# Weight products of a one-core decode block: the weights as moving operand in four column tiles, c loaded as rows, a 256 KB last load

## The chip, the cores and the metric

The kernel runs on one core of one Trainium2 chip. The metric is the device time of one execution in microseconds (us), lower is better. A median is given with the lowest and the highest run. A profiled execution has a span, from its first to its last instruction; the time is some 1.8 us longer than the span of the same execution (426.25 and 424.5 us before).

Engines: PE = TensorE (matmul), PEld = its weight loads, DVE = VectorE, ACT = ScalarE, POOL = GpSimd, SP = SyncE.

## The reference, cut to what matters

```
mod = (silu(c) @ w_mod)                          # c [2, 1024], w_mod [1024, 6144], bf16
sa, ca, ga, sb, cb, gb = six parts of mod
h = layernorm(x) * (1 + ca) + sa                 # x [2, 1, 1024]
q = h @ wq                                       # wq [1024, 4096]
o = softmax(q @ K^T * 128**-0.5) @ V             # caches [2, 4, 32768, 128], 32 query heads
x = x + ga * (o @ wo)                            # wo [4096, 1024]
h = layernorm(layernorm(x) * (1 + cb) + sb)
x = x + gb * (gelu(h @ w1 + b1) @ w2 + b2)       # w1 [1024, 3584], w2 [3584, 1024]
```

Each batch row gives one token, so every product with a weight matrix has only two rows. The caches are 134 MB and the weights 44 MB: everything is read once, and there is little to compute on it.

## The kernel before

A single stream of loads of 1 to 2 MB fills a ring of buffers in the on-chip memory. SP issues them in a fixed order, each as soon as its place in the ring is free. The stages are: w_mod (8 loads), wq (4), K and V (64), wo (4), w1 (4), w2 (4). Loads of the weights, and the order of w_mod's rows:

```
    wm_v = w_mod.rearrange("(p k) n -> p k n", k=KT8)
    for k in range(KT8):
        add(("wmod", k), [6 * DM], wm_v[:, k, :], k * 12 * KB)
    # ... wq, K and V, wo, w1
    w2_v = B_w2.rearrange("(q p j) n -> p q (j n)", p=128, j=4)
    for k, off in enumerate((80, 112, 128, 144)):
        lo, hi = 2 * k, min(2 * k + 2, 7)
        add(("w2", k), [hi - lo, 4 * DM], w2_v[:, lo:hi, :], off * KB)   # three of 2 MB, the last 1 MB
```

c is loaded so that each of the 128 partitions gets its own 16 bytes of each row. The weights are the stationary operand of each matmul, in blocks of 128 by 128, and the two columns of the input are moved past them. The result stands in columns, which is the form that the next stage wants:

```
    T.dma("act", lambda e: e.dma_start(c_sb[:, :, :], c.rearrange("b (p k) -> p b k", k=KT8)), ...)

    for k in range(KT8):                                   # w_mod; wq, wo and w1 alike
        for j in range(NMOD):                              # 48
            pe(lambda e, ...: e.matmul(psS[0][:, 2 * j:2 * j + 2], lhsT=w[:, j * 128:(j + 1) * 128], rhs=siluT[:, :, k], ...))

    for q in range(7):                                     # w2, the end of the kernel
        it = need("w2", q // 2)
        for j in range(4):
            for k in range(KT8):
                pe(lambda e, ...: e.matmul(psO[:, 2 * k:2 * k + 2], lhsT=w[:, q % 2, j * DM + k * 128:j * DM + (k + 1) * 128],
                                           rhs=gT[:, 4 * q + j, :], ...))
    dve(mT = psO * mod(5));  dve(res_bf = mT + x1b)        # shortened
    pe(turn res_bf into rows);  dve(copy to res16);  store
```

## Time and profile before

| | before |
|---|---|
| median, lowest to highest | 426.06 us, 426.01 to 426.18 (3 runs) |
| span of the profiled execution | 424.5 us |
| read from memory | 178.28 MB, 420 GB/s over the span |
| last load has landed / end of the span | 420.48 / 424.5 us |

No engine is busy for more than 68%, but the DMA engines are 90% busy or more in every slice except the first and the last. The loads bound the kernel. Two queues carry instructions rather than data: 16 packets of 16 KB on one, and 8 packets of 8 KB on the other.

The costliest groups, two weight stages of before (line, engine, operation, output <- input, shape, count | busy us, mean ns of one | idle time before them and its releaser):

```profile
L448 PE MATMUL psS<-siluT,wmod 128*128 128x2 bf16 x384 | 11.0, 165 | 8.6 <-DMA wmod<-in_w_mod_dram 8.6
...
L647 PE MATMUL psO<-gT,w 128*128 128x2 bf16 x224 | 6.6, 165 | 9.5 <-DMA w<-in_B_w_dram 9.5
```

The idle time of PE in both stages ends with a load.

Windows of 1 us at the end of before. Columns: window, its length, then busy time and count of PE, PEld, DVE, ACT and POOL, granted clock of PE, DMA share, GB/s.

```profile
416.00:417.00 1.00, 0.00 (x0) 0.00 (x0) 0.00 (x0) 0.00 (x0) 0.00 (x0) 0.50 0.89 369
417.00:418.00 1.00, 0.00 (x0) 0.00 (x0) 0.00 (x0) 0.00 (x0) 0.00 (x0) 0.50 0.61 246
418.00:419.00 1.00, 0.91 (x34) 0.91 (x35) 0.00 (x0) 0.00 (x0) 0.00 (x0) 0.50 0.50 213
419.00:420.00 1.00, 0.96 (x36) 0.87 (x33) 0.00 (x0) 0.00 (x0) 0.00 (x0) 0.50 0.24 98
```

The DMA share falls from 0.89 to 0.24 before the last load is complete. The engines do not finish together. The page counts 16 DMA engines, and in this trace each large load shows 16 semaphore increments at different times; here each is read as one engine's end. The offsets of those of the last w2 load, in us after the first of them, sorted (worked out from the semaphore records of the trace):

```
before, first at 416.79: 0 .1 .2 .3 .4 .8 1.6 1.9 3.0 3.1 3.1 3.2 3.2 3.2 3.2 3.7
```

The first w_mod load has a spread of 0.35 us, this one 3.7 us. PE waited for the last of the 16: its products of the third w2 load started at 418.09 us and those of the last at 420.52 us, each 0.04 to 0.05 us after the 16th increment (418.04 and 420.48 us). The end of the chain of waits of before (start us, us, what):

```profile
391.30 29.17 DMA w<-in_B_w_dram
420.48 0.05 issue
420.52 1.03 PE psO L647 x32
...
421.57 0.18 DVE mT L651
...
421.78 0.24 DVE res_bf L652
...
422.07 0.29 PE psM L653
...
422.38 0.28 DVE res L655
```

After the last landing at 420.48 us come 32 matmuls, four small steps and the store. From here on, "tail" is the time from the last landing to the end of the span: 4.0 us in before. So the span is last landing plus tail, and each part can be read alone.

### The profile page before, as it was taken

Reading aid. Unit: us, or ns where it says so; the run is one execution under the profiler, and the core shown is the slowest. Engines: PE = TensorE matmul, PEld = TensorE weight load, DVE = VectorE, ACT = ScalarE, POOL = GpSimd, SP = SyncE. Lnnn points to the kernel's source line nnn. Section 1 sums busy time; section 2 is a strip of 40 time slices with the busy share of each in tenths; the row PEclk is TensorE's granted clock in tenths of the full one; section 3 lists DMA queues with packets and bytes.
Section 4 is the critical chain, followed back from the end, with each engine's and each line's share of the span. In section 5 each row is a group of like instructions: output and inputs, shape, how many; then the busy total and the mean of one; then the engine's idle time right before and its main releaser. Section 6 shows DMA issues by size and latency. Waiting matters only on the chain.

```text
span 424.5 us, 13364 instructions
## 1 busy us (share of the span) xinstructions
PE 287.6 (68%) x6035; PEld 252.8 (60%) x6035; DVE 162.8 (38%) x340; ACT 155.1 (37%) x266; POOL 2.8 (1%) x17
## 2 busy tenths in 40 slices
PE   0633369768997789578867857895878681544644
PEld 0633368766875778477766837784867661243643
DVE  0200027535674466146535624661555343102100
ACT  1100016428556348143734543481438335100100
POOL 1000000000000000000000000000000000000000
PEclk9999999969999889888969898897889886855555
DMA  8999999999999999999999999999999999999994
GB/s 329 429 425 422 435 426 426 431 424 433 428 434 429 434 431 430 431 431 432 432 432 429 433 426 435 428 432 432 429 434 428 432 432 430 431 428 420 426 427 176
DMA packets 14470, 178.61 MB, mean 421 GB/s; under 512 B 1767, under 2 KB 1774, under 8 KB 2798
## 3 DMA queue, kind: packets, MB, share of 16 engines
q1 hardware_dynamic: 14112, 178.27, 98.6%
q8 instruction: 16, 0.26, 0.2%
q10 hardware_dynamic: 334, 0.02, 0.1%
q14 instruction: 8, 0.07, 0.0%
HBM read 178.28 MB, written 0.00 MB: 420 GB/s over the span
## 4 chain that ended last, share of the span: by engine, by line
DMA 79%; PE 17%; ACT 1%; SPq 1%; DVE 1%; issue 1%; DVEq 0%; ACTq 0%
DMA K<-in_A_k_cache_dram 59%; PE psKT L477 11%; DMA wo<-in_A_wo_dram 8%; DMA w<-in_B_w_dram 7%; DMA wmod<-in_w_mod_dram 5%; PE psS L489 3%; PE psO L519 1%; SPq L374 1%; ACT KT_sb L481 1%; ACT E_sb L510 0%; PE psS L613 0%; PE psO L647 0%; ACT L510 0%; DVE KT_sb L483 0%; PE psM L423 0%
## 5 line engine op out<-in xcount | busy, mean ns | idle before, releaser
L477 PE MATMUL psKT<-ident,K 128*128 128x128 bf16 x2048 | 175.5, 238 | 39.7 <-DMA K<-in_A_k_cache_dram 39.7
L477 PEld LDWEIGHTS psKT<-ident,K 128*128 128x128 bf16 x2048 | 134.5, 106 | 50.3 <-DMA K<-in_A_k_cache_dram 46.2
L481 ACT ACTIVATE KT_sb<-psKT 128x1024 bf16<-128x1024 bf16 x96 | 97.8, 1019 | 169.5 <-PE psKT L477 169.3
L483 DVE COPY KT_sb<-psKT 128x1024 bf16<-128x1024 bf16 x160 | 108.3, 689 | 117.4 <-PE psKT L477 116.2
L489 PE MATMUL psS<-qcur,KT_sb 128*128 128x8 bf16 x2048 | 88.8, 168 | 10.8 <-ACT KT_sb L481 7.1
L489 PEld LDWEIGHTS psS<-qcur,KT_sb 128*128 128x128 bf16 x2048 | 80.1, 99 | 16.5 <-ACT KT_sb L481 9.3
L519 PE MATMUL psO<-V,E_sb 128*32 128x512 bf16 x512 | 34.4, 394 | 4.1 <-DMA V<-in_A_v_cache_dram 3.3
L510 ACT ACTIVATE E_sb<-S_sb,negm 128x256 bf16<-128x256 f32 x64 | 32.3, 505 | 9.7 <-DVE negm L506 8.8
L494 DVE TENSOR_REDUCE m1c<-S_sb 128x8 f32<-128x512 f32 x32 | 21.9, 686 | 16.4 <-ACT S_sb L493 15.1
L493 ACT ACTIVATE S_sb<-psS 128x512 f32<-128x512 f32 x32 | 19.0, 593 | 15.0 <-PE psS L489 15.0
L519 PEld LDWEIGHTS psO<-V,E_sb 128*32 128x32 bf16 x512 | 11.3, 98 | 14.3 <-DMA V<-in_A_v_cache_dram 4.1
L448 PE MATMUL psS<-siluT,wmod 128*128 128x2 bf16 x384 | 11.0, 165 | 8.6 <-DMA wmod<-in_w_mod_dram 8.6
L448 PEld LDWEIGHTS psS<-siluT,wmod 128*128 128x128 bf16 x384 | 10.8, 104 | 9.0 <-DMA wmod<-in_w_mod_dram 9.0
L456 PE MATMUL psO<-hT,wq 128*128 128x2 bf16 x256 | 7.5, 165 | 12.5 <-DMA wq<-in_A_wq_dram 12.5
L613 PE MATMUL psS<-atT,wo 128*128 128x2 bf16 x256 | 7.5, 165 | 12.2 <-DMA wo<-in_A_wo_dram 12.2
L613 PEld LDWEIGHTS psS<-atT,wo 128*128 128x128 bf16 x256 | 7.1, 104 | 13.1 <-DMA wo<-in_A_wo_dram 13.1
L456 PEld LDWEIGHTS psO<-hT,wq 128*128 128x128 bf16 x256 | 7.1, 104 | 12.8 <-DMA wq<-in_A_wq_dram 12.8
L425 ACT ACTIVATE stat<-stat 128x2 f32<-128x2 f32 x3 | 0.6, 203 | 36.9 <-DVE stat L424 36.9
L647 PE MATMUL psO<-gT,w 128*128 128x2 bf16 x224 | 6.6, 165 | 9.5 <-DMA w<-in_B_w_dram 9.5
L647 PEld LDWEIGHTS psO<-gT,w 128*128 128x128 bf16 x224 | 6.3, 104 | 9.8 <-DMA w<-in_B_w_dram 9.8
L510 ACT ACTIVATION_READ_ACCUMULATOR E_sb<-S_sb,negm 128x1 f32 x64 | 12.1, 189 | 0.0
L629 PE MATMUL psS<-h2T,w 128*128 128x2 bf16 x224 | 7.8, 172 | 3.1 <-DMA w<-in_B_w_dram 1.9
(85 smaller groups left out, 85.7 us busy)
## 6 DMA issues: line engine op xcount, KB each, us to landing
K<-in_A_k_cache_dram SPq DMA_DIRECT2D x32, 2048.0 KB, 31.8
V<-in_A_v_cache_dram SPq DMA_DIRECT2D x32, 2048.0 KB, 35.4
wmod<-in_w_mod_dram SPq DMA_DIRECT2D x8, 1536.0 KB, 18.0
wq<-in_A_wq_dram SPq DMA_DIRECT2D x4, 2048.0 KB, 37.8
wo<-in_A_wo_dram SPq DMA_DIRECT2D x4, 2048.0 KB, 27.3
w<-in_B_w_dram SPq DMA_DIRECT2D x4, 1792.0 KB, 37.7
w<-in_B_w_dram SPq DMA_DIRECT2D x3, 2048.0 KB, 30.8
w<-in_B_w_dram SPq DMA_DIRECT2D x1, 1024.0 KB, 29.2
```

What stands on the lines that cost most here:

```text
L448: pe(lambda e, w=it.view, j=j, k=k: e.matmul(psS[0][:, 2 * j:2 * j + 2], lhsT=w[:, j * 128:(j + 1) * 128], rhs=siluT[:, :, k], start=(k == ...
L456: pe(lambda e, w=it.view, h=h, k=k: e.matmul(psO[:, 2 * h:2 * h + 2], lhsT=w[:, k % 2, h * 128:(h + 1) * 128], rhs=hT[:, k, :], start=(k = ...
L477: pe(lambda e, kq=kq, jj=jj, w=it.view, t=t: e.transpose(psKT[kq][:, jj * 128:(jj + 1) * 128], w[:, t, :], ident[:, :]), reads=[it.reg, "i ...
L481: act(lambda e, src=src: e.activation(KT_sb[g8][:, :, :], src, ACT.Copy), reads=[f"psKT{kq}"], writes=[f"KT_sb{g8}"], sem=f"ev{cc}_{g8}")
L483: dve(lambda e, src=src: e.tensor_copy(KT_sb[g8][:, :, :], src), reads=[f"psKT{kq}"], writes=[f"KT_sb{g8}"], sem=f"ev{cc}_{g8}")
L489: pe(lambda e, t=t, jj=jj: e.matmul(ps[:, t * HPG:(t + 1) * HPG], lhsT=KT_sb[g8][:, jj, :], rhs=qcur[:, :], start=True, stop=True), reads= ...
L493: act(lambda e: e.activation(Sc, ps[:, :].rearrange("p (t h) -> p h t", h=HPG), ACT.Copy), reads=[preg], writes=[f"S_sb{i % 2}_{cc}"], sem ...
L494: dve(lambda e: e.tensor_reduce(m1c[:, :, cc], Sc, AX.X, ALU.max), reads=[f"S_sb{i % 2}_{cc}"], writes=[f"m1c{cc}"])
L510: act(lambda e: e.activation(E_sb[:, :, h, :], S_sb[j][:, h, :].rearrange("p (u t) -> p u t", t=4), ACT.Exp, bias=negm[:, h:h + 1], scale= ...
L519: pe(lambda e, t4=t4, tg=tg, q=q: e.matmul(psO[32 * q:32 * q + 32, :], lhsT=E_sb[:, tg // 4, :, :].rearrange("p h t -> p (h t)"), rhs=it.v ...
L613: pe(lambda e, w=it.view, g=g, j=j, k=k: e.matmul(psS[0][:, 2 * k:2 * k + 2], lhsT=w[:, j, k * 128:(k + 1) * 128], rhs=atT[g][:, j, :], st ...
L647: pe(lambda e, w=it.view, q=q, j=j, k=k: e.matmul(psO[:, 2 * k:2 * k + 2], lhsT=w[:, q % 2, j * DM + k * 128:j * DM + (k + 1) * 128], rhs= ...
```

## The change

The intent: make the weights the moving operand, 512 columns at a time, against a stationary operand of 32 columns, of which two hold the input. Four such products go to four column tiles of the array at once. This cuts PE's instructions for the weights from 1,344 matmuls to 360. In the P.V stage of before (line 519), which had this form already, four matmuls start within about 10 ns of each other at clock 1.0 (12 ns at most), and within 14 ns at 0.5; a group of four follows the last after 216 ns and 426 ns (medians).

The price is that results come as rows. In this kernel they are copied out of PSUM and turned into columns by matmuls with a small selection matrix, in float32 except for q. The core of the diff (declarations, padding of the inputs to 32 columns, wq and w1 cut):

```diff
-    wm_v = w_mod.rearrange("(p k) n -> p k n", k=KT8)
+    wm_v = w_mod.rearrange("(k p) n -> p k n", k=KT8)
 ...
-    for k, off in enumerate((80, 112, 128, 144)):
-        lo, hi = 2 * k, min(2 * k + 2, 7)
-        add(("w2", k), [hi - lo, 4 * DM], w2_v[:, lo:hi, :], off * KB)
+    for k, off in enumerate((80, 112, 128)):
+        add(("w2", k), [2, 4 * DM], w2_v[:, 2 * k:2 * k + 2, :], off * KB)
+    add(("w2", 3), [3 * DM], w2_v[:, 6, 0:3 * DM], 144 * KB)
+    add(("w2", 4), [DM], w2_v[:, 6, 3 * DM:4 * DM], 150 * KB)
 ...
-    T.dma("act", ... c_sb[:, :, :], c.rearrange("b (p k) -> p b k", k=KT8)), key="ld_c", ...)
+    T.dma("act", ... c16[:, :], c.rearrange("b (k p) -> (b k) p", p=128)), key="ld_c", ...)
 ...
     for k in range(KT8):
         it = need("wmod", k)
-        for j in range(NMOD):
-            pe(... e.matmul(psS[0][:, 2 * j:2 * j + 2], lhsT=w[:, j * 128:(j + 1) * 128], rhs=siluT[:, :, k], ...)
+        for ch in range(12):
+            n, q = ch // 4, ch % 4
+            pe(... e.matmul(bank[n][32 * q:32 * q + 32, :], lhsT=inT[:, k, :], rhs=w[:, ch * 512:(ch + 1) * 512], ...)
+    # three copies of 512 columns to SBUF, 12 float32 matmuls that turn them into columns
 ...
-    for q in range(7):
+    for q in range(6):
         it = need("w2", q // 2)
         for j in range(4):
-            for k in range(KT8):
-                pe(... e.matmul(psO[:, 2 * k:2 * k + 2], lhsT=w[:, q % 2, ...], rhs=gT[:, 4 * q + j, :], ...)
+            for hf in range(2):
+                t = 2 * (j % 2) + hf
+                pe(... e.matmul(psS[0][32 * t:32 * t + 32, :], lhsT=gT[:, 4 * q + j, :],
+                                rhs=w[:, q % 2, j * DM + hf * 512:j * DM + (hf + 1) * 512], ...)
+    load_row("dve", psS[0], "psS0", 3)
+    for j in range(4):                                    # the last 1 MB in the old form
+        it = need("w2", 3 if j < 3 else 4)
+        if j == 3:
+            to_columns(psO, "psO", 3, False, False)       # turn of w2's row: four float32 matmuls
+        for k in range(KT8):
+            pe(... e.matmul(psO[:, 2 * k:2 * k + 2], lhsT=w[:, lo:lo + 128], rhs=gT[:, 24 + j, 0:2], ...)
```

The two bias loads also move, from the start to after the attention loop, and one of them is split in four.

## The prediction

> What bounds the kernel. The load stream: the page gives 178.28 MB read at 421 GB/s, and its DMA row is 9 in every slice but the first and the last; the windows view gives 427 to 432 GB/s from 40 us to 415 us. Loads are issued some 31 us ahead (K), so no compute stage starves the queue: PE is 35 to 60% busy in the weight stages, waiting for a load each time. Only three things move the time: when the stream starts, how evenly its 16 engines finish, and what follows the last landing.
>
> 1. Even finish. In the windows view the DMA share falls to 0.89, 0.61, 0.50, 0.24 in the single microseconds from 416 to 420. The semaphore increments of the last w2 load run from 416.79 to 420.48 us. This spread is 0.3 us at first (wmod 0) and grows by about 1.5 us on one engine after each 16 KB packet of the instruction queue (16 on the page). At the end eight engines stand at 0 to 0.8 us or with one fetch at 1.6 to 1.9, the rest with two at 3.0 to 3.7: fetches go round about eight engines. Counted from the built programs, PE has about 4,095 instructions of 64 B, 16 pages of 16 KB; after, about 2,250, 8.8 pages (weight matmuls fall from 1,344 to 360). With 8 fetches, one per engine, I expect a spread of 1.6 to 2.2 us and the last landing 1.6 us earlier (1.3 to 2.0).
>
> 2. Head. c as 256 packets of 16 B lasts until 10.6 us, [...] but costs each engine only 0.15 to 0.3 us. Gain 0.2 us. PE starts wmod at 6 us instead of 15.7: worth nothing, the ring is prefilled.
>
> 3. PE in the weight stages. Old: 64 weight loads in 1.79 us. New: 16 matmuls of 512 columns; the same form in the last P.V stage (line 519) takes 427 ns per four at clock 0.5, 216 at 1.0. So 1.7 us per 2 MB against a load every 4.9 us: worth nothing. [...] Row copies and float32 turns add some 3 us after wo and 5 us after w1 (a float32 pass is 0.23 us at clock 0.5, line 418); gT comes near 411.5 instead of 406.7, after w2's first landing, but PE catches up before the third. Off the critical path.
>
> 4. Tail. Before, 32 matmuls follow the last landing (1.05 us); the end comes 4.0 us after it. After, 8 follow, but the turn of w2's row stands before them in PE's order: the third w2 load lands 2.4 us before the last, its 16 matmuls end 0.5 us before it, the copy of 512 float32 takes about 0.6 us (estimate from the 0.69 us reduction of line 494), then four float32 matmuls, eight passes of 0.23 us, 1.8 us. PE ends 2.3 us after the last landing instead of 1.1: plus 1.2 us (0.8 less if the clock is up).
>
> Sum: -0.2 - 1.6 + 1.2 = -0.6 us: 425.4 us, range 423.9 to 426.8. Faster by over 2%: 0.01; within: 0.98; slower: 0.01.
>
> What would show it: 8 or 9 instruction-queue packets instead of 16 (DMA queues); DMA share near 1 until 416.5, dropping faster (windows); last w2 landing near 418.6; the chain of waits ending in the turn of w2's row, not in a load.
>
> Wrong if: two fetches fall on one engine (1.4 us slower), the clock rises in w2 (0.8 faster), the turn is hidden, or the late bias loads put engines behind.

What the trace of before shows for some of its figures: c's 256 packets of 16 bytes took 9 ns each, which is 0.14 us for each of 16 engines if they were spread evenly (an estimate from these figures); 16 packets of 16 KB over the 4,095 counted instructions give 64 B for one; and at line 418 a float32 matmul stands as two passes that start 0.23 us apart at clock 0.5. The 0.8 us for a higher clock was the author's estimate.

## More of the kernel before

DVE's other work, which matters later: in each of the eight attention rounds DVE copies 20 of the 32 groups of turned K out of PSUM (`EVAC_PATTERN`, five of eight), ACT the other 12. DVE also takes the maximum of the scores, in four parts and once more over the four.

From the page of the kernel before: its span; busy time of each engine, share of the span and count of instructions; DMA share in 40 slices, in tenths (9 is 90% or more); two of the DMA queues with packets, MB and share; and bytes read.

```profile
span 424.5 us, 13364 instructions
PE 287.6 (68%) x6035; PEld 252.8 (60%) x6035; DVE 162.8 (38%) x340; ACT 155.1 (37%) x266; POOL 2.8 (1%) x17
...
DMA  8999999999999999999999999999999999999994
...
q8 instruction: 16, 0.26, 0.2%
...
q14 instruction: 8, 0.07, 0.0%
HBM read 178.28 MB, written 0.00 MB: 420 GB/s over the span
```

## The result, and the profile after

Ratios here and below are the mean time of one kernel's fast runs over the mean of the other's fast runs of the same rounds, so they are not quite the ratio of the medians quoted.

| | before | after |
|---|---|---|
| median, lowest to highest (4 runs each) | 426.03 us, 425.90 to 426.18 | 427.38 us, 427.30 to 427.42 |
| ratio to before, 95% interval | | 1.0031, 1.0014 to 1.0049 |
| span of the profiled execution | 424.5 us | 425.5 us |
| last landing | 420.48 us | 420.21 us |
| tail, last landing to end | 4.0 us | 5.3 us |

The kernel is 1.35 us slower, within 2%, and outside the predicted range of 423.9 to 426.8 us. In the profiled executions the last landing came 0.27 us sooner and the tail became 1.3 us longer. The page after:

```profile
span 425.5 us, 11554 instructions
PE 301.5 (71%) x5116; PEld 236.0 (55%) x5116; DVE 166.9 (39%) x347; ACT 156.8 (37%) x269; POOL 4.9 (1%) x23
...
q8 instruction: 9, 0.15, 0.1%
q14 instruction: 8, 0.07, 0.0%
```

The 16 KB instruction packets fell from 16 to 9, as predicted (the ninth came after the last landing). The 8 KB packets remained 8. PE became busier (301.5 us against 287.6), not less busy. The groups of the new weight stages:

```profile
L451 PE MATMUL psS<-wmod,inT 128*32 128x512 bf16 x64 | 8.0, 593 | 13.4 <-DMA wmod<-in_w_mod_dram 13.4
L641 PE MATMUL psS<-wo,atT 128*32 128x512 bf16 x64 | 7.6, 627 | 12.0 <-DMA wo<-in_A_wo_dram 12.0
```

PE still waits for the load in these stages; the form of the product is worth nothing there. The windows at the end:

```profile
416.00:417.00 1.00, 0.00 (x0) 0.00 (x0) 0.00 (x0) 0.00 (x0) 0.00 (x0) 0.50 0.84 346
417.00:418.00 1.00, 0.23 (x4) 0.14 (x8) 0.00 (x0) 0.00 (x0) 0.00 (x0) 0.50 0.62 250
418.00:419.00 1.00, 1.00 (x12) 0.33 (x8) 0.00 (x0) 0.00 (x0) 0.00 (x0) 0.50 0.24 94
419.00:420.00 1.00, 1.00 (x22) 0.39 (x15) 0.28 (x1) 0.00 (x0) 0.00 (x0) 0.50 0.06 23
```

In the last of these microseconds the DMA share is 0.06, that is one engine of sixteen. The increments of the last load show the same:

```
before, first at 416.79: 0 .1 .2 .3 .4 .8 1.6 1.9 3.0 3.1 3.1 3.2 3.2 3.2 3.2 3.7
after,  first at 416.64: 0 .2 .4 .5 .8 .8 1.6 1.6 1.8 1.9 2.1 2.1 2.1 2.2 2.5 3.6
```

The seven engines at 3.0 to 3.2 us are gone, as wanted. One engine at 3.6 us has remained, and it is the one that the last load waits for. The chain of waits after:

```profile
387.77 29.96 DMA w<-in_B_w_dram
417.73 0.04 issue
417.77 1.93 PE psS L708 x15
...
419.72 0.70 DVE S_sb L650
...
420.47 1.87 PE psO L654 x8
422.34 0.23 PE psO L719 x8
...
422.59 0.19 DVE mT L722
```

The chain no longer goes back to the last load, which lands at 420.21 us. It comes from the third w2 load (417.73) over 16 matmuls, the copy of the row and its turn. The turn's eight float32 passes last until 422.34 us; only then come the eight matmuls for the last 256 KB. PE's last product ends 2.34 us after the last landing, against 1.07 us in before.

### The profile page after: what moved, and what is told of

The parts are those of the page before. It is cut to its first block, busy times and chain, and to the rows that moved or that the text cites. A ratio compares the mean times of both kernels' runs of the same rounds, so it can differ in the third digit from the quotient of the medians.

```text
span 425.5 us, 11554 instructions
## 1 busy us (share of the span) xinstructions
PE 301.5 (71%) x5116; PEld 236.0 (55%) x5116; DVE 166.9 (39%) x347; ACT 156.8 (37%) x269; POOL 4.9 (1%) x23
## 4 chain that ended last, share of the span: by engine, by line
DMA 79%; PE 18%; ACT 1%; SPq 1%; issue 0%; DVE 0%; DVEq 0%
DMA K<-in_A_k_cache_dram 59%; PE psKT L500 11%; DMA wo<-in_A_wo_dram 8%; DMA w<-in_B_w_dram 7%; DMA wmod<-in_w_mod_dram 5%; PE psS L512 3%; PE psO L542 1%; SPq L377 1%; ACT KT_sb L504 1%; PE psS L708 0%; PE psS L641 0%; PE psO L654 0%; ACT E_sb L533 0%; DVE S_sb L650 0%; PE psM L523 0%
## 5 line engine op out<-in xcount | busy, mean ns | idle before, releaser
L500 PE MATMUL psKT<-ident,K 128*128 128x128 bf16 x2048 | 173.4, 236 | 36.8 <-DMA K<-in_A_k_cache_dram 34.4
L500 PEld LDWEIGHTS psKT<-ident,K 128*128 128x128 bf16 x2048 | 132.6, 106 | 48.7 <-DMA K<-in_A_k_cache_dram 42.0
L542 PE MATMUL psO<-V,E_sb 128*32 128x512 bf16 x512 | 39.0, 435 | 5.3 <-DMA V<-in_A_v_cache_dram 4.6
L451 PE MATMUL psS<-wmod,inT 128*32 128x512 bf16 x64 | 8.0, 593 | 13.4 <-DMA wmod<-in_w_mod_dram 13.4
L641 PE MATMUL psS<-wo,atT 128*32 128x512 bf16 x64 | 7.6, 627 | 12.0 <-DMA wo<-in_A_wo_dram 12.0
L472 PE MATMUL psS<-wq,inT 128*32 128x512 bf16 x64 | 7.5, 627 | 7.0 <-DMA wq<-in_A_wq_dram 6.0
L451 PEld LDWEIGHTS psS<-wmod,inT 128*32 128x32 bf16 x64 | 1.2, 108 | 19.0 <-DMA wmod<-in_w_mod_dram 18.8
L641 PEld LDWEIGHTS psS<-wo,atT 128*32 128x32 bf16 x64 | 1.8, 128 | 16.7 <-DMA wo<-in_A_wo_dram 14.6
L650 DVE COPY S_sb<-psS 128x512 f32<-128x512 f32 x2 | 1.4, 692 | 22.1 <-PE psS L641 13.0
L563 PE MATMUL psM<-msum,hmat 128*128 128x128 f32 x16 | 4.2, 346 | 7.5 <-DVE msum L557 7.5
L459 DVE COPY S_sb<-psS 128x512 f32<-128x512 f32 x1 | 0.7, 692 | 21.5 <-PE psS L451 21.5
```

Source lines behind the costliest of these rows:

```text
L451: pe(lambda e, w=it.view, k=k, ch=ch, n=n, q=q: e.matmul(bank[n][32 * q:32 * q + 32, :], lhsT=inT[:, k, :], rhs=w[:, ch * 512:(ch + 1) * 512],
L472: pe(lambda e, w=it.view, k=k, ch=ch, n=n, q=q: e.matmul(bank[n][32 * q:32 * q + 32, :], lhsT=inT[:, k, :], rhs=w[:, k % 2, ch * 512:(ch + ...
L500: pe(lambda e, kq=kq, jj=jj, w=it.view, t=t: e.transpose(psKT[kq][:, jj * 128:(jj + 1) * 128], w[:, t, :], ident[:, :]), reads=[it.reg, "i ...
L542: pe(lambda e, t4=t4, tg=tg, q=q: e.matmul(psO[32 * q:32 * q + 32, :], lhsT=E_sb[:, tg // 4, :, :].rearrange("p h t -> p (h t)"), rhs=it.v ...
L641: pe(lambda e, w=it.view, g=g, j=j, hf=hf, q=q: e.matmul(psS[0][32 * q:32 * q + 32, :], lhsT=atT[g][:, j, :], rhs=w[:, j, hf * 512:(hf + 1 ...
```

## The theory, and how pages are followed

The result leaves two questions: whether the turn is the whole loss in the tail, and which engine it is that ends last.

*Instruction pages.* The trace of before shows packets of the kind "instruction" while the kernel runs: 16 of 16 KB, at 21.1 to 421.5 us, and 8 of 8 KB, at 88.9 to 354.4 us. One such packet is called a page here. The built programs have about 4,095 PE instructions before and 2,250 after, and the page of each kernel shows 16 and 9 packets of 16 KB: in before that is one for 256 instructions, and 2,250 would be 8.8 of these. So they are read as PE's. The 8 KB packets are read as pages of the other engines. At the start of four of them DVE's count of records in the trace is 65, 200, 329 and 453 in before, and 67, 197, 328 and 456 in after, so one comes about every 128 instructions. The author's estimate from this is the 64th, the 192nd, the 320th and the 448th. Three belong to ACT in the same way (its records then count 67, 203 and 319 in before). The one left, at 354.4 us, fits neither count and is put down to SP.

*What a page costs.* The offset of an engine can be followed from load to load, because the increments of successive loads keep their order until something delays one engine. In before and after a PE page put one engine about 1.5 us behind (in before from 1.59 to 3.15 us, seen at the landing at 381.3 us), a DVE page about 0.95 us (list below), an ACT page about 0.65 us (in before from 0.83 to 1.48 us at 210.7 us, and from 1.37 to 2.01 us at 293.3 us). The delay stayed, but for a drift of some 0.1 us (in before from 2.10 us at 166.9 us to 2.01 us at 244.7 us), while the stream didn't pause. The clearest trace is the experiment old_row_order below, where one engine shows four jumps:

```
old_row_order: DVE pages fetched at 83.7, 159.9, 239.2, 318.4 us
               jumps of one engine, seen at the landings at 87.5, 165.5, 244.1, 322.7 us: 1.06 0.95 0.96 0.90
before:        DVE pages fetched at 88.9, 163.3, 243.7, 323.6 us
               jumps of one engine, seen at the landings at 94.1, 166.9, 249.6, 327.9 us: 0.95 0.97 0.96 0.94
after:         DVE pages fetched at 84.9, 160.5, 239.1, 318.4 us
               jumps of one engine, seen at the landings at 87.8, 165.7, 244.1, 322.7 us: 0.97 0.97 0.97 0.95
```

So in these runs PE's pages went round about eight engines, but DVE's all fell on the same one. Four of them make about 3.8 us. The limit of this: packets in the trace do not name their DMA engine, and where two offsets cross in the list the identities cannot be told apart for certain (in after the engine passes another at about 1.06 us and at about 1.85 us). So the reading had to be tested by changing the number of pages.

*Theory D*: the engine with DVE's four pages ends last in both kernels; PE's pages in before hide just below it. *Rivals*: (R1) the spread at the start, which grew from 0.35 to about 1 us with the change of c's load or of w_mod's row order, is what holds the end; (R2) PE's pages still set the end, two of them on one engine. Theory D was formed after the first four runs; the expectation of more_pe, one of these, still speaks of PE's pages alone.

## The experiments

Fourteen kernels ran, in four groups, each on one chip with its own runs of before (medians 426.05, 426.19, 426.09 and 425.99 us). After itself was not run again in these groups: where its 427.38 us is the measure below, the comparison goes across groups, whose runs of before differ by up to 0.2 us. Results agreed with the reference in all. One kernel (old_row_order) computes a wrong result and still passed the comparison, so the comparison cannot tell whether the w_mod product is right in any of these kernels.

Summary (last landing, tail and spread from the profiled execution):

| kernel | median us (range) | ratio to before, 95% | last landing | tail | spread, last load |
|---|---|---|---|---|---|
| turn_early | 425.73 (425.49 to 426.05) | 0.9993, 0.9976 to 1.0010 | 420.31 | 3.4 | 3.29, next 2.0 |
| before_split | 425.48 (425.42 to 425.56) | 0.9985, 0.9969 to 1.0002 | 420.29 | 3.3 | 3.54 |
| small_packets | 428.05 (427.42 to 428.79) | 1.0050, 1.0033 to 1.0066 | 420.53 | 5.3 | 3.33, next 2.0 |
| more_pe | 427.61 (427.60 to 427.80) | 1.0036, 1.0020 to 1.0053 | 420.48 | 5.3 | 3.63, six at 3.1 to 3.3 |
| after_no_max | 426.51 (426.30 to 426.61) | 1.0006, 0.9989 to 1.0023 | 419.47 | 5.3 | 2.85 |
| before_no_max | 425.73 (425.71 to 426.07) | 0.9992, 0.9975 to 1.0008 | 419.95 | 4.0 | 3.21 |
| old_row_order | 427.58 (427.37 to 428.38) | 1.0031, 1.0014 to 1.0048 | 420.28 | 5.3 | 3.44, next 1.9 |
| more_dve | 435.80 (434.83 to 436.41) | 1.0224, 1.0207 to 1.0241 | 428.54 | 5.3 | 4.19, next 1.8 |
| no_max_four_pages | 427.42 (427.28 to 427.50) | 1.0030, 1.0015 to 1.0046 | 420.40 | 5.3 | 3.42, next 2.1 |
| pattern_only | 427.55 (427.11 to 429.05) | 1.0041, 1.0024 to 1.0059 | 420.61 | 5.3 | 3.63, next 2.9 |
| best_after | 424.77 (424.70 to 424.92) | 0.9970, 0.9956 to 0.9983 | 419.57 | 3.4 | 2.46 |
| best_before | 425.26 (425.11 to 425.29) | 0.9981, 0.9967 to 0.9994 | 419.87 | 3.4 | 3.07, eight at 2.8 to 3.1 |
| fifth_page_after | 428.46 (428.36 to 429.28) | 1.0056, 1.0040 to 1.0073 | 421.19 | 5.1 | 4.61, next 2.2 |
| fifth_page_before | 426.78 (426.70 to 426.94) | 1.0018, 1.0002 to 1.0035 | 421.04 | 4.0 | 4.31, next 3.3 |

The tail takes only three values. It is 4.0 us with a last load of 1 MB, 3.3 to 3.4 us with a last load of 256 KB and no turn after it, and 5.1 to 5.3 us with the turn after it. The rest of every difference is the last landing.

### The tail: turn_early and before_split

turn_early is after, with only the first two loads of w2 (q 0 to 3) in rows. Their turn happens while PE waits for the third load, and the rest is done in the old form:

```diff
-    for q in range(6):
+    for q in range(4):
         # ... products into rows as before
     load_row("dve", psS[0], "psS0", 3)
+    to_columns(psO, "psO", 3, None, True)
+    for q in range(4, 6):
+        it = need("w2", q // 2)
+        # ... 64 matmuls of the old form, weights stationary
     for j in range(4):
         it = need("w2", 3 if j < 3 else 4)
-        if j == 3:
-            to_columns(psO, "psO", 3, False, False)
```

> Changed kernel, but only w2 rows q 0 to 3 go through row form; their turn into columns is issued while PE waits for the third w2 load, and q 4 to 6 keep the old form. My theory (the float32 turn stands between the last landing and the end): PE ends about 0.4 us after the last landing instead of 2.34, time falls by about 1.9 us, from 427.4 to 425.5, with the last landing unchanged at 420.2 (within 0.3). Rival (the tail is long for another reason, such as the low clock or the extra load's completion, and the turn merely fills a wait): under 0.7 us gained. Result stays correct.

The chain of waits of turn_early, towards its end:

```profile
387.87 29.96 DMA w<-in_B_w_dram
417.83 0.05 issue
417.88 1.82 PE psO L719 x64
...
419.72 1.03 PE psO L726 x32
...
420.77 0.18 DVE mT L729
```

The turn is gone from it. PE ends 0.44 us after the last landing instead of 2.34, while the landing itself is the same (420.31 against 420.21). The median is 1.65 us below that of after (1.9 was expected). So the turn of w2's row accounts for the loss in the tail.

before_split is before with only the last load cut:

```diff
-    for k, off in enumerate((80, 112, 128, 144)):
-        lo, hi = 2 * k, min(2 * k + 2, 7)
-        add(("w2", k), [hi - lo, 4 * DM], w2_v[:, lo:hi, :], off * KB)
+    for k, off in enumerate((80, 112, 128)):
+        add(("w2", k), [2, 4 * DM], w2_v[:, 2 * k:2 * k + 2, :], off * KB)
+    add(("w2", 3), [1, 3 * DM], w2_v[:, 6:7, 0:3 * DM], 144 * KB)
+    add(("w2", 4), [1, DM], w2_v[:, 6:7, 3 * DM:4 * DM], 150 * KB)
```

> Kernel before, with only the last w2 load cut into 768 KB and 256 KB. Theory: only 8 matmuls follow the last landing instead of 32, tail 0.75 us shorter, landing unchanged: 425.3. Rival (one more load costs as much as it saves): 426.0.

Its tail is 3.3 us against 4.0, and its median 0.57 us below that of before in the same group. This part of the change helps alone, and in after the turn hid it. Its chain of waits:

```profile
417.82 0.05 issue
417.87 2.86 PE psO L649 x96
```

From the third landing of w2 on, PE works through 96 matmuls without a gap, until 0.44 us after the last landing (420.29 us). So here, as in turn_early, PE no longer waits for the last landing but for the third load. Both come late by the same engine.

### Spread at the start: small_packets and old_row_order

small_packets is after plus an unused load of c in the old form, 256 packets of 16 bytes:

```diff
+    T.dma("act", lambda e: e.dma_start(c_sb[:, :, :], c.rearrange("b (p k) -> p b k", k=KT8)), key="ld_cs", writes=["c_sb"])
```

> Changed kernel plus an unused load of c in 256 packets of 16 B on ACT's queue, as the kernel before has it. In the changed kernel the 16 increments of the first wmod load spread over 1.1 us, before over 0.35. Theory 1 (the small packets, [...] evened the engines' start): spread after the first loads falls to about 0.4, the last landing comes 0.3 to 0.7 us earlier, time 426.8 to 427.2. Theory 2 (the spread at the start comes from the other reading order of w_mod, contiguous rows): spread stays near 1.1, time 427.4 to 427.6.

The spread of the w_mod loads stayed at 0.74 to 0.87 us, as in turn_early, which lacks the small packets (0.84 to 0.89), and the last landing did not come sooner (420.53). The median is above both expectations, by the two runs whose time is 2.6 and 3.0 us longer than their span; the spans are 425.6 to 425.9 us. The small packets were not what had kept the engines together in before. They are slow to arrive, though: in before c's 4 KB landed only at 10.61 us, and at 4.68 us in after, as rows. In the trace of before the 256 packets start between 2.32 and 9.81 us, about 16 of them in every 0.46 us, while the packets of 12 KB beside them took 0.48 us each (mean of the first 20 us).

old_row_order is after with the old order of w_mod's rows, which gives a wrong mod (the `-` line is that of after):

```diff
-    wm_v = w_mod.rearrange("(k p) n -> p k n", k=KT8)
+    wm_v = w_mod.rearrange("(p k) n -> p k n", k=KT8)
```

> Changed kernel, but w_mod is read in the old order of rows (row 8p+k instead of 128k+p to partition p), so the result is wrong on purpose; all instructions are the same. Theory (contiguous rows spread the engines' start): the increments of the first w_mod loads spread over 0.3 to 0.5 us instead of 0.85 to 1.1, landing up to 0.5 us earlier, time 426.9 to 427.3. Rival (the spread at the start has another cause, e.g. the missing small packets): spread stays 0.85 or more, time 427.4.

The spread of the w_mod loads fell to 0.29 to 0.49 us (in after it was 0.91 to 1.09 us, in before 0.31 to 0.41 us until the first page): the row order makes it. But the time did not change (427.58 against 427.38), and one engine still ended alone at 3.44 us, with the next at 1.9. The expectation that this brings the landing forward was a miss. So R1 falls: the engine with DVE's pages was among the early ones at the start of this run (0.08 us) and became the last.

### PE's pages: more_pe

768 matmuls whose result nobody reads are added to the w_mod and wq stages of after:

```diff
+        for r in range(64):      # in w_mod; 32 in wq
+            pe(lambda e, ...: e.matmul(psM[:, 200:202], lhsT=w[:, (r % 32) * 128:(r % 32 + 1) * 128], rhs=inT[:, k, 0:2], start=True, stop=True), ...)
```

> Changed kernel plus 768 unused two-column matmuls in PE's waits of the w_mod and wq stages: 1,536 more PE instructions, 6 pages of 16 KB. Theory (every page fetched puts one DMA engine about 1.4 us behind the others, in turn on eight engines): 15 instruction-queue packets of 16 KB instead of 9, and where the slowest engine is among those hit, the spread of the last landing grows from 3.6 to about 5 us and the time by about 1.4 us, to 428.8; if it is not among them, unchanged. Rival (the number of fetches doesn't matter to the end, since the stream is bound by its bytes): 427.4, spread 3.6.

```profile
q8 instruction: 14, 0.23, 0.2%
```

Fourteen pages came instead of nine (15 were expected). Six engines stand at 3.1 to 3.3 us and one at 3.6, the median rose by 0.23 us, and the last landing came 0.27 us later. The spread of 3.6 us is what the rival said, but it belongs to another engine than in after, as the lists before and after the PE page of 401.8 us show (the engines above 1.8 us):

```
more_pe, load landing from 399.66: 1.85 2.21 3.10 3.18 3.24 3.26 3.36 3.37
         load landing from 404.58: 1.81 3.07 3.15 3.21 3.23 3.30 3.33 3.72
```

The engine at 2.21 us, which had gone from 0.87 to 2.39 us at the PE page of 53.4 us, rose to 3.72 us and ended last, at 3.63. DVE's engine, followed through its four pages, is among the six. So this run does not rule R2 out: with 14 PE pages an engine with two of them ends last, by 0.3 us. That it gives 3.6 us again is chance. For after itself R2 fails on its count of pages: its eight PE pages before the last landing appear as eight jumps of 1.4 to 1.7 us on eight engines, none of which ends last. That rests on following the offsets; the runs that follow change DVE's pages themselves.

### DVE's pages: more_dve, then after_no_max and before_no_max

more_dve was to add two DVE pages by 256 copies of one element in DVE's program:

```diff
+    for _ in range(256):
+        dve(lambda e: e.tensor_copy(dum[:, :], half[:, 0, 0:1]), reads=["half"], writes=["dum"])
```

> Changed kernel plus 256 unused one-column DVE copies while DVE waits for w_mod: two more 8 KB pages of DVE. Theory: six DVE pages instead of four, each puts one engine 0.95 us behind; those that fall on the engine that ends last already make the landing and the time 0.95 us later each: 428.3 (one) or 429.2 (both), 427.4 only if both fall on others. Rival: 427.4.

It was badly made. Each copy took about 0.19 us, so DVE was busy until some 60 us, the first K tiles were consumed late, and the ring ran empty of free places. Its windows, columns as above:

```profile
50.00:60.00 10.00, 0.00 (x0) 0.00 (x0) 8.17 (x54) 0.00 (x0) 0.00 (x0) 1.00 1.02 436
65.00:70.00 5.00, 3.93 (x26) 3.21 (x29) 0.78 (x4) 0.00 (x0) 0.00 (x0) 1.00 0.24 102
70.00:75.00 5.00, 4.21 (x56) 1.75 (x48) 0.32 (x1) 0.60 (x1) 0.00 (x0) 1.00 0.66 206
```

The stream fell to 102 GB/s between 65 and 70 us. In the pause the late engines caught up: the spread was 2.24 us in the load landing from 66.2 us and 0.59 us in the one from 77.9 us. So the landing tells nothing clean about pages. Inconclusive.

The opposite was cleaner: fewer DVE instructions. after_no_max and before_no_max leave out the maximum before exp (the scores of these inputs are small enough, as the comparison showed; it is not a general kernel) and give four of eight copies of turned K to ACT:

```diff
-EVAC_PATTERN = ("dve", "act", "dve", "act", "dve", "dve", "act", "dve")
+EVAC_PATTERN = ("dve", "act", "dve", "act", "dve", "act", "dve", "act")
 ...
-            dve(lambda e: e.tensor_reduce(m1c[:, :, cc], Sc, AX.X, ALU.max), ...)
-    # and softmax_1, softmax_2, softmax_3; negm is set to zero once
```

DVE then has 418 and 400 instructions, below the counts of 453 (before) and 456 (after) at which the fourth page came. ACT does more in exchange and gets a fourth page of its own, so the page of after_no_max still counts 8 packets of 8 KB:

```profile
q14 instruction: 8, 0.07, 0.0%
```

By the counts of records at their starts (DVE's 67, 196 and 320; ACT's 68, 191, 320 and 447) three are DVE's and four ACT's, with one left for SP. The count of the queue alone does not show what was changed.

> Changed kernel with fewer VectorE instructions: no maximum is taken before exp (the scores are small, so the result stays correct; negm is 0) and one eviction of eight goes from DVE to ACT: 418 DVE instructions instead of 563, so three 8 KB pages of DVE instead of four (a page at about the 64th, 192nd, 320th, 448th instruction). Followed by the increments of each load, a DVE page puts one DMA engine 0.95 us behind, a PE page 1.55, an ACT page 0.65, and in the changed kernel the engine that ends last (3.6 us after the first, 1.1 after the next) has one PE page and two DVE pages. Theory: spread of the last landing falls to 2.5 to 2.9 us, landing 0.7 to 1.1 us earlier, time 426.3 to 426.7. Rival (the spread comes from something else, or the end does not follow it): 427.2 to 427.6.

> The same cut of DVE instructions in the kernel before (400 instead of 548). There the engine that ends last has four DVE pages and no PE page (3.8 us of pages), but seven others have two PE pages each and end only 0.4 to 0.7 us sooner. Theory: the spread falls from 3.7 to 3.2 to 3.4 and no further, time 425.6 to 425.8. Rival: the same gain as in the changed kernel (0.7 to 1.1), or none.

In after the last landing came 0.74 us sooner and the median fell by 0.87 us (the runs of before in the two groups differ by 0.16 us). In before it gained less: 0.46 us of median within its group, because the seven engines with two PE pages, at 2.9 to 3.2 us, then ended last; DVE's engine stood at 2.8 us. Both are what theory D says. One clause of the expectation of after_no_max was wrong, though: it gave the engine that ends last in after one PE page and two DVE pages. Followed through the trace it has DVE's four and no PE page. The forecast needed only that the fourth DVE page falls on it, so the number came out all the same.

### Is it the page, or what was removed? no_max_four_pages and pattern_only

after_no_max removes work as well as a page. The two edits were therefore done apart. No maximum alone leaves 481 DVE instructions, the new pattern alone 500; both are above the 453 and 456 at which the fourth page came, so four pages were expected.

> Changed kernel without the maximum before exp, eviction pattern as it was: 481 DVE instructions instead of 563, which still passes the 448th, so four DVE pages as before. Theory (whole pages count, not the work): spread stays 3.4 to 3.7 us, time 427.2 to 427.6. Rival (after_no_max gained because DVE and PE had less to do): about 426.6.

> Changed kernel with one eviction of eight moved from DVE to ACT, maximum kept: 500 DVE instructions, four DVE pages. Theory: spread stays 3.4 to 3.7 us, time 427.2 to 427.6. Rival (the balance of evictions made the gain of after_no_max): about 426.6.

Medians of 427.42 and 427.55 us, against 427.38 of after: neither part alone is worth anything. In no_max_four_pages one engine stands alone at 3.42 us, the next at 2.1. Only the two together, with 418 instructions and three pages, gave 0.87 us. ACT's fourth page came in pattern_only too (it shows 9 packets of 8 KB) and changed nothing. It is not the work, it is the page.

### One page more: fifth_page_after and fifth_page_before

After has 563 DVE instructions and before 548; a fifth page would come at about 576, an estimate from the steps of about 128 between the first four. 64 and 72 one-element copies cross that, and cost DVE only 12 to 14 us at the start (at 0.19 us each):

```diff
+    for _ in range(64):          # 72 in before, reading m16
+        dve(lambda e: e.tensor_copy(dum[:, :], half[:, 0, 0:1]), reads=["half"], writes=["dum"])
```

> Changed kernel plus 64 unused one-column DVE copies (0.19 us each) in DVE's wait for w_mod, 12 to 25 us: 627 DVE instructions instead of 563, a fifth page (from the 576th) near 390 us. Theory: spread 4.3 to 4.6 us instead of 3.6, landing about 0.95 us later, time 428.2 to 428.6. Rival: 427.4.

> Kernel before plus 72 such copies, 18 to 32 us: 620 DVE instructions, a fifth DVE page near 395 us. Theory (in the kernel before, too, the engine with the DVE pages ends last): spread 4.4 to 4.7 us instead of 3.7, time 426.8 to 427.1. Rival (the engines with two PE pages end last, as the prediction had it, and DVE pages fall elsewhere): spread 3.7, time 426.1.

The offsets of the last load:

```
after:             0 .2 .4 .5 .8 .8 1.6 1.6 1.8 1.9 2.1 2.1 2.1 2.2 2.5 3.6
fifth_page_after:  0 .3 .4 .5 .7 .9 1.5 1.8 2.0 2.0 2.1 2.2 2.2 2.2 2.2 4.6
before:            0 .1 .2 .3 .4 .8 1.6 1.9 3.0 3.1 3.1 3.2 3.2 3.2 3.2 3.7
fifth_page_before: 0 .1 .2 .3 .4 .7 1.7 1.9 2.9 3.1 3.1 3.1 3.1 3.2 3.3 4.3
```

The fifth page is there in both runs:

```profile
q14 instruction: 9, 0.07, 0.0%
```

Only the last engine moved, by 1.0 us in after and 0.6 us in before. The jump itself was 0.91 and 0.95 us (pages fetched at 357.7 and 358.8 us); in fifth_page_before the engine stood some 0.2 us lower before it (3.50 us) than in before. The medians rose by 1.08 us (0.85 us by the medians of the spans, 425.55 to 426.4) and, within its group, by 0.79 us. fifth_page_before landed just below its expected spread (4.4 to 4.7) and median (426.8 to 427.1), but it shows what the increments alone could not: in the kernel before, too, the engine with DVE's pages ends last.

The timeline of PE in fifth_page_after (start us, us, line, output <- input, shapes, count):

```profile
420.60 0.80 PE L723 MATMUL psO<-gT,w 128*128 128x2 bf16 x24 [0.27 <-DMA w<-in_B_w_dram]
421.26 1.85 PE L658 MATMUL psO<-half,S_sb 128*128 128x4 f32 x8
422.97 0.35 PE L723 MATMUL psO<-gT,w 128*128 128x2 bf16 x8
```

Even with the last landing 1 us later, at 421.19 us, the turn starts after it, since the third and the fourth w2 load came 1 us later too. A late stream does not hide the turn.

### Both kernels without the two faults: best_after and best_before

best_after is turn_early with DVE cut to 443 instructions, best_before is before_split with the same cut to 444. The maximum stays; it is taken once over all scores instead of in four parts and once more. Four of eight copies of turned K go to ACT, and one more per round. Five small operations move to POOL:

```diff
-            dve(lambda e: e.tensor_reduce(m1c[:, :, cc], Sc, AX.X, ALU.max), ...)
-        dve(lambda e: e.tensor_reduce(m1[:, :], m1c[:, :, :], AX.X, ALU.max), ...)
+        dve(lambda e: e.tensor_reduce(m1[:, :], S_sb[i % 2][:, :, :], AX.X, ALU.max), ...)
-        if EVAC_PATTERN[g8] == "act":
+        if EVAC_PATTERN[g8] == "act" or (g8 == 4 and cc == 3):      # in best_after only
 ...
-        dve(lambda e: e.tensor_copy(rsum16[:, :, :], ...))
+        T.inst("pool", lambda e: e.tensor_copy(rsum16[:, :, :], ...))
         # hmat, diag and the two steps of x1b likewise
```

> turn_early, with 443 DVE instructions: one maximum per group in place of four and a combining one, some evictions to ACT, the diagonal, the row-sum broadcast and the bias product to POOL. Three DVE pages. Theory: turn_early (425.7) less 0.7 to 0.9 us: spread about 2.5 us, landing 419.4, time 424.7 to 425.1, below the kernel before (426.1). Rival (pages don't set the end): 425.7.

> before_split with the same cut of DVE instructions, 444: three DVE pages, but the 16 PE pages stay, two on each of seven or eight engines. Theory: these hold the spread at 3.2 us, time 425.0 to 425.3, so 0.2 to 0.4 us behind best_after; that difference is what the change's fewer PE instructions are worth once nothing else hides them. Rival: equal to best_after or faster.

The windows at the end of best_after:

```profile
417.00:418.00 1.00, 0.86 (x32) 0.86 (x33) 0.00 (x0) 0.00 (x0) 0.00 (x0) 0.50 0.68 277
418.00:419.00 1.00, 1.00 (x39) 0.95 (x37) 0.00 (x0) 0.00 (x0) 0.00 (x0) 0.50 0.37 125
419.00:420.00 1.00, 1.00 (x33) 0.91 (x32) 0.00 (x0) 0.00 (x0) 0.00 (x0) 0.50 0.02 6
```

Its last landing is 419.57 us, 0.64 us sooner than in after, and its tail 3.4 us. At 424.77 us it beats both kernels: 2.6 us less than after, 1.3 us less than before in its group, with an interval that leaves out 1. It is still within 2%. best_before is 0.49 us slower, and all five runs of one lie below all five of the other. There the seven engines with two PE pages and DVE's engine with three of its own end together, at 2.8 to 3.1 us. (Both kernels show 9 packets of 8 KB. The author put two of them down to a fourth page of ACT and one of POOL, added while DVE's fourth went; that they fell on other engines was not shown apart from the spreads of 2.46 and 3.07 us.) So with the DVE page gone the changed kernel is ahead by 0.3 us of landing (419.57 against 419.87) and 0.5 us of time (0.3 us by the medians of the spans, 423.0 against 423.3). That fits the fewer PE pages, but the two kernels differ in more than these, so what the pages alone are worth is not shown.

## Why the prediction was wrong, and where it was right

1. *Even finish: wrong, and this is the step that failed.* The prediction gave the spread of 3.7 us to the engines with two 16 KB fetches, and so expected 1.6 to 2.2 us, and a last landing 1.6 us earlier, from 8 fetches. The fetches fell as predicted (16 to 9), and the engines that had two came 1 us sooner. But the spread of the last load is 3.57 us and the landing came 0.27 us earlier. The last engine was another one, which carries DVE's four 8 KB pages at about 0.95 us each. It was only 0.4 to 0.7 us behind the others in before, and the change does not touch it. Even without it the spread would have been 2.5 us, above the prediction's: the next engine began about 1.06 us behind with the new row order, which the prediction did not foresee, and had one PE page. The queue with the 8 packets stood on the page of before, and the prediction did not use it. The list of 16 offsets showed one engine apart from the group, too; it was counted to the group.
2. *Head: about nothing, as expected, but not separated.* c landed at 4.68 us. PE did not start on w_mod at 6 us but at 10.25 us, because x landed at 7.03 us and x's turn and the first layernorm stand before it in PE's order. That is worth nothing, as the prediction said of the stage. The predicted gain of 0.2 us was not isolated by any run. A wider start spread came with the new row order (0.35 to about 1 us), and cost nothing by old_row_order, where DVE's engine ends last all the same.
3. *PE in the weight stages: right.* gT came at 410.44 us (predicted 411.5), and the second w2 load's products started at 412.88 us, close behind its landing. The idle time of PE in the new stages ends with loads.
4. *Tail: right.* PE ended 2.34 us after the last landing (predicted 2.3), and the chain runs through the turn of w2's row. turn_early removed it and gave 1.65 us. The tail grew by 1.3 us against a predicted 1.2.

The sum shows it: expected −0.2 − 1.6 + 1.2 = −0.6 us; found, by spans, −0.27 + 1.3 = +1.0 us (the medians of the times differ by 1.35 us; the profiled run of before was 0.2 us slower than its median). The term of −1.6 us is what was missing. Of the listed risks, "two fetches fall on one engine" was the nearest, but it named the wrong engine's instructions.

What stays open: why a DVE page whose packet took 0.31 us puts its engine 0.95 us behind, and a PE page with a packet of 0.9 us about 1.5 us; which DMA engine is which, since the lists of offsets don't name them; whether the moved bias loads cost anything; and what the tail would be at a higher granted clock than the 0.50 seen in both kernels.

## What to carry to other kernels

This kernel was bound by its loads, and its span was the last landing plus the tail (420.48 + 4.0 us before, 420.21 + 5.3 us after). In such a case list the 16 increments of the last load, follow the last engine back from load to load to what put it behind (in more_pe the same 3.6 us belonged to another engine), and count a gain only as far as the next engine in that list. In the tail, ask of each new step not how long it lasts but whether it stands after the last landing in its engine's order; work of the same length can go before it (turn_early, 1.65 us). Here an engine's count of instructions cost time where its busy share did not: DVE was 39% busy in after, and 64 copies more cost 1.08 us of time (0.85 us of span). A few instructions fewer helped only when a page went with them: with 563, 500 and 481 DVE instructions the medians were 427.38, 427.55 and 427.42 us, with 418 it was 426.51 us.
